# Storing the leftover tokens of a fused attention and two-layer kernel by one transfer a batch, from two issuing engines

## The chip, the cores and the metric

The kernel runs on one core of one Trainium2 chip. Its time is the device time of one execution in microseconds (us). The engines are named as the profile names them: PE (matrix multiplication) with PEld (its weight loads), DVE, ACT and POOL (the three engines for elementwise work), and SP, which here only issues transfers. Sixteen DMA engines move data between the on-chip memory and DRAM.

## The reference

Four batches (B) of eight heads, 576 tokens (S) a batch. Linear attention with 128 random features gives 2304 rows of 512 values; two gated feed-forward layers with 2048 hidden columns follow. The output is 2304 x 512 in fp32, its row being `batch * 576 + token`.

```python
q_p, k_p = (phi(q_s), phi(k_s))             # phi: exp of a projection on omega, less a maximum
kv = np.einsum('bhsm,bhsd->bhmd', k_p, v)
num = np.einsum('bhsm,bhmd->bhsd', q_p, kv)
out = num / den                              # attention; then rows (b s), columns (h d)

h = x @ w_in                                 # layer one
x = (h * np.clip(h + 3.0, 0.0, 6.0) / 6.0) @ w_out
h = x @ w_in                                 # layer two, with weights of its own
out = (h * (1.0 / (1.0 + np.exp(-1.702 * h)))) @ w_out
```

## The kernel before

A batch of 576 tokens is cut into 512 main tokens (`SM`) and 64 leftover tokens (`SL`). The main tokens of each batch are a block of their own, i = 0 to 3; the 4 x 64 leftover tokens of all batches together are a fifth block, i = B = 4, of 256 tokens. Token t of that block belongs to batch t // 64, so tokens 0 to 127 are batches 0 and 1, and 128 to 255 batches 2 and 3.

A first stretch computes the attention of batch 0, then the units of the two layers run in the order layer, batch, chunk of 128 hidden columns (16 chunks). `emit_h` (line 439) multiplies by `w_in` and applies the gate, `emit_o` (line 501) multiplies by `w_out` and adds up in PSUM, two units later. fp32 values are split into two parts, and three products are taken. The attention of the next batch is slipped in between, step by step, through `side()`.

The last pass of layer two handles batch 3 and the leftover block together (`SEGS[3]`). At its end (`tail`) the order of `emit_o` is written out by hand: the main block's last chunk first, then the leftover block's last two. The leftover block has two accumulators, d = 0 and d = 1, of 128 tokens by 512 columns each; both are finished last in the program.

`put` takes an accumulator from PSUM into the tile `ob` (line 522 on ACT for even d, line 520 on DVE for odd d) and stores it: line 524 for layer one, line 529 for a main block of layer two (128 rows of the output that follow each other), and line 534 for the leftover block. Line 534 is reached twice. All stores of `put`, and all other transfers, are issued by SP, in program order. The tile `ob` has six buffers in this stage (`lp`), so that no store waits there for an earlier one. Line 717 is the end of the program, where SP waits for the transfers still under way, and all engines meet.

Of the kernel before, what the change touches and what calls it, by code (L numbers as in the profile page):

```python
# [46 lines left out]
def performer_moe_kernel(  # L47
# [13 lines left out]
    nc = tc.nc  # L61
# [9 lines left out]
    SM = R * P  # L71
    SL = lv.shape[1] // 2
    S = SM + SL
# [392 lines left out]
    def emit_o(l, n, c, side):  # L466
# [5 lines left out]
        for c, i, N in parts:  # L472
# [7 lines left out]
            for d, ps in enumerate(oacc[l, i]):  # L480
# [27 lines left out]
                if c == NC - 1:  # L508
                    put(l, i, d, ps, per)
# [4 lines left out]
    def put(l, i, d, ps, per):  # L514
        pool, bufs = (gp, 2) if lp is None else (lp, 6)
        ob = pool.tile([P, SM], F32, tag="ob", bufs=bufs, name="ob")
        ps = ps.rearrange("p e s -> p (e s)")
        sc = 1.0 / 6.0 if l == 0 else 1.0
        if d % 2:
            nc.vector.tensor_scalar(out=ob, in0=ps, scalar1=sc, scalar2=None, op0=ALU.mult)  # L520
        else:
            nc.scalar.activation(out=ob, in_=ps, func=AF.Copy, scale=sc)
        if l == 0:
            nc.sync.dma_start(
                out=xs[i][d * per:(d + 1) * per].rearrange("e p s -> p e s"),
                in_=ob.rearrange("p (e s) -> p e s", e=per),
            )
        elif i < B:
            nc.sync.dma_start(
                out=out[i * S + d * P:i * S + (d + 1) * P, :],  # L530
                in_=ob,
            )
        else:
            nc.sync.dma_start(
                out=out.rearrange("(b s) e -> b s e", s=S)[2 * d:2 * d + 2, SM:S, :],
                in_=ob,
            )

    def split_x(t, x, kk):
        nc.scalar.copy(x[:, 0, kk, :], t[:, kk, :])  # L540
# [18 lines left out]
    for n in range(WARM):  # L559
        nc.tensor.matmul(  # L560
            out=ps.rearrange("p a m -> p (a m)"),
# [6 lines left out]
    for e in range(2):  # L568
# [5 lines left out]
            out=bd_lo[rows, e, :],  # L574
# [147 lines left out]
```

## Time and profile before

| | us |
|---|---|
| median of 3 runs | 982.69 |
| lowest and highest of the three | 978.67, 982.96 |
| the profiled execution | 980.37 |
| its span, first to last instruction | 978.6 |
| last stretch, 965.10 to the end, without work on any engine | 13.5 |

The profile's page gives the busy time of each engine, its share in 40 slices of the span, the DMA queues and the chain of work that ended last. Other views group the instructions by line, list them in order of time, tell what each waited for, and count in any stretch the DMA packets, the bytes moved and the share of the sixteen DMA engines that was busy. Times in them count from the span's start.

### The profile page before, as it was taken

The numbers are of one execution on the slowest core, as the hardware profiler recorded it, in microseconds if no ns is written. First come the engines' busy times: TensorE is split into PE (matmuls) and PEld (weight loads), VectorE is DVE, ScalarE is ACT, GpSimd is POOL, SyncE is SP. The second block draws the span as 40 slices with busy tenths as digits, with TensorE's granted clock in tenths as the row PEclk, the third lists the DMA queues.
The fourth block names the chain that finished last, engine by engine and source line by source line (L and its number), as shares of the span: only waits on it lengthen the run. The fifth ranks groups of instructions, "written<-read, shape, count | busy, mean of one in ns | idle before, by whom it ended". The sixth has DMA issues, their size and how long they took to land.

```text
span 978.6 us, 14409 instructions
## 1 busy us (share of the span) xinstructions
PE 946.1 (97%) x5626; PEld 783.8 (80%) x5626; DVE 477.7 (49%) x845; ACT 415.5 (42%) x868; POOL 152.4 (16%) x127
## 2 busy tenths in 40 slices
PE   8799999999999999999999999999999999999994
PEld 6678777788877778778888888888888888888883
DVE  7988988886776875333222222223223222322221
ACT  5976776675655665342222322222123212221221
POOL 0212322334443343030000101020002000000000
PEclk9999999999999999999999999999999999999997
DMA  6666677977788865246333384446335443422301
GB/s 196 249 226 224 214 258 247 370 266 270 270 306 281 288 227 204 86 151 211 120 124 128 129 264 140 134 148 212 131 130 175 130 144 114 150 67 86 108 1 64
DMA packets 54775, 177.23 MB, mean 181 GB/s; under 512 B 5812, under 2 KB 7476, under 8 KB 54708
## 3 DMA queue, kind: packets, MB, share of 16 engines
q1 hardware_dynamic: 54708, 176.32, 52.9%
q8 instruction: 44, 0.72, 0.3%
q14 instruction: 23, 0.19, 0.1%
HBM read 138.55 MB, written 37.75 MB: 180 GB/s over the span
## 4 chain that ended last, share of the span: by engine, by line
PE 74%; DVE 7%; DMA 7%; POOL 5%; ACT 3%; issue 3%; SPq 0%; POOLq 0%; ACTq 0%
PE ps L439 34%; PE o L501 34%; DMA ws1i<-wsn 4%; POOL wsn L211 3%; DVE w L205 3%; PE ps L225 2%; DMA ws1o<-wsn 2%; POOL w L202 2%; DVE mx L231 1%; PE ps L329 1%; ACT w L187 1%; PE ps L292 1%; DVE wtop L193 1%; ACT e L233 0%; DMA qk<-in_qk_dram 0%
## 5 line engine op out<-in xcount | busy, mean ns | idle before, releaser
L439 PE MATMUL ps<-x,wss 128*128 128x512 f32 x1152 | 287.3, 394 | 3.4 <-ACT wss L210 1.9
L439 PEld LDWEIGHTS ps<-x,wss 128*128 128x128 f32 x1152 | 212.2, 188 | 48.0 <-ACT wss L210 3.5
L457 DVE TENSOR_TENSOR ga<-ga,ps 128x512 f32<-128x512 f32 x80 | 50.8, 635 | 252.4 <-ACT ga L456 252.4
L456 ACT ACTIVATE ga<-ps 128x512 f32<-128x512 f32 x80 | 44.4, 554 | 252.3 <-PE ps L439 252.3
L501 PE MATMUL o<-gs,wss 128*128 128x512 f32 (+1 forms) x600 | 137.3, 375 | 1.3 <-ACT gs L459 1.0
L460 DVE TENSOR_TENSOR gs<-ga,gs 128x512 fp32r<-128x512 f32 (+1 forms) x160 | 109.1, 697 | 51.1 <-ACT gs L459 48.1
L501 PE MATMUL o<-wss,gs 128*128 128x512 f32 x540 | 129.8, 390 | 0.0
L501 PEld LDWEIGHTS o<-gs,wss 128*128 128x128 f32 x600 | 102.2, 189 | 20.1 <-ACT gs L459 1.3
L501 PEld LDWEIGHTS o<-wss,gs 128*128 128x128 f32 x540 | 100.7, 188 | 20.5
L459 ACT CAST gs<-ga 128x512 fp32r<-128x512 f32 (+1 forms) x160 | 91.7, 579 | 43.6 <-DVE ga L457 32.4
L202 POOL TENSOR_TENSOR w<-w,wpow 128x512 f32<-128x512 f32 x64 | 77.7, 1234 | 168.0 <-DVE wpow L197 129.1
L452 DVE SCALAR_TENSOR_TENSOR ga<-ga,ps 128x512 f32<-128x512 f32 x80 | 50.1, 629 | 109.3 <-ACT ga L451 109.1
L439 PE MATMUL ps<-x,wsh 128*128 128x512 f32 x384 | 94.7, 393 | 0.5 <-ACT wsh L210 0.5
L451 ACT ACTIVATE ga<-ps,three 128x512 f32<-128x512 f32 x80 | 51.6, 648 | 101.7 <-PE ps L439 101.5
L439 PEld LDWEIGHTS ps<-x,wsh 128*128 128x128 f32 x384 | 70.9, 188 | 15.8 <-ACT wsh L210 0.7
L501 PE MATMUL o<-gs,wsh 128*128 128x512 f32 (+1 forms) x360 | 82.9, 374 | 0.6 <-ACT gs L459 0.4
L205 DVE TENSOR_TENSOR w<-w,wtop 128x512 f32<-128x512 f32 x64 | 75.3, 1188 | 16.3 <-POOL w L202 16.3
L501 PE MATMUL o<-wsh,gs 128*128 128x512 f32 x324 | 78.5, 390 | 0.0
L233 ACT ACTIVATE e<-ps,mx 128x128 f32<-128x128 f32 x220 | 63.4, 386 | 24.6 <-DVE mx L231 24.4
L501 PEld LDWEIGHTS o<-gs,wsh 128*128 128x128 f32 x360 | 61.6, 189 | 12.2 <-ACT gs L459 1.0
L501 PEld LDWEIGHTS o<-wsh,gs 128*128 128x128 f32 x324 | 60.4, 188 | 12.3
L541 POOL TENSOR_TENSOR x<-xr,x 128x512 fp32r<-128x512 f32 x16 | 22.2, 1417 | 264.2 <-ACT x L540 264.2
(123 smaller groups left out, 963.3 us busy)
## 6 DMA issues: line engine op xcount, KB each, us to landing
wss<-ws1i SPq DMA_DIRECT2D x48, 512.0 KB, 3.2
wss<-ws1o SPq DMA_DIRECT2D x40, 512.0 KB, 3.3
wss<-ws0i SPq DMA_DIRECT2D x36, 512.0 KB, 4.9
wraw<-in_w_in_dram SPq DMA_DIRECT2D x32, 512.0 KB, 4.5
wraw<-in_w_out_dram SPq DMA_DIRECT2D x32, 512.0 KB, 5.6
wss<-ws0o SPq DMA_DIRECT2D x30, 512.0 KB, 4.2
ws1i<-wsn SPq DMA_DIRECT2D x16, 512.0 KB, 3.5
ws1o<-wsn SPq DMA_DIRECT2D x16, 512.0 KB, 3.0
```

Of the source, the lines that this page charges most:

```text
L202: nc.gpsimd.tensor_tensor(out=w[:, cols], in0=w[:, cols], in1=q[:, cols], op=ALU.mult)
L205: nc.vector.tensor_tensor(out=wj, in0=wj, in1=a[:, j * DM:(j + 1) * DM], op=ALU.add)
L211: (nc.vector if l == 0 else nc.gpsimd).tensor_tensor(out=s[:, 1], in0=wj, in1=s[:, 0].bitcast(F32), op=ALU.subtract)
L233: act = nc.scalar.activation(out=e[:, r, :], in_=ps[:, r, :], func=AF.Exp, bias=mx[:, r:r + 1])
L439: nc.tensor.matmul(out=ps, lhsT=w[:, wi, kk, :], rhs=x[:, xi, kk, :], start=(m == 0), stop=(m == 3 * NK - 1),)
L451: nc.scalar.activation(out=g, in_=ps, func=AF.Relu, bias=three)
L452: nc.vector.scalar_tensor_tensor(out=g, in0=g, scalar=6.0, in1=ps, op0=ALU.min, op1=ALU.mult)
L456: nc.scalar.activation(out=g, in_=ps, func=AF.Sigmoid, scale=1.702)
L457: nc.vector.tensor_tensor(out=g, in0=g, in1=ps, op=ALU.mult)
L459: nc.scalar.copy(s[:, 0, :], g)
L460: nc.vector.tensor_tensor(out=s[:, 1, :], in0=g, in1=s[:, 0, :].bitcast(F32), op=ALU.subtract)
L501: last = nc.tensor.matmul(out=ps[:, e, :], lhsT=lhsT, rhs=rhs, start=(c == 0 and m == 0 and per == 1), stop=(c == NC - 1 and m == 2 and e ...
```

## The change

The leftover block's store of one accumulator (128 rows of `ob`, two batches of 64 rows each, which lie 576 rows apart in the output) becomes two stores of 64 rows. The one for the even batch is issued by SP, the one for the odd batch by ACT. Line 534 is reached for d = 0 and d = 1, so two transfers become four.

```diff
         else:
-            nc.sync.dma_start(
-                out=out.rearrange("(b s) e -> b s e", s=S)[2 * d:2 * d + 2, SM:S, :],
-                in_=ob,
-            )
+            for e, eng in enumerate((nc.sync, nc.scalar)):
+                r0 = (2 * d + e) * S + SM
+                eng.dma_start(out=out[r0:r0 + SL, :], in_=ob[e * SL:(e + 1) * SL, :])
```

## Rows read from the trace of the kernel before

**Rows 1.** The page: span, busy us of PE with its share, PE and DMA by slices

```profile
span 978.6 us, 14409 instructions
PE 946.1 (97%) x5626; PEld 783.8 (80%) x5626; DVE 477.7 (49%) x845; ACT 415.5 (42%) x868; POOL 152.4 (16%) x127
...
PE   8799999999999999999999999999999999999994
...
DMA  6666677977788865246333384446335443422301
```

**Rows 2.** Busy us (x instructions) in four stretches, then granted clock, DMA share, GB/s

```profile
0.00:662.00 662.00, 643.72 (x4204) 530.06 (x4205) 394.85 (x711) 341.70 (x731) 146.92 (x123) 1.00 0.62 213
662.00:956.18 294.18, 294.18 (x1388) 247.27 (x1388) 79.42 (x129) 70.83 (x132) 5.49 (x4) 1.00 0.36 119
956.18:965.10 8.92, 8.19 (x37) 6.42 (x35) 3.42 (x6) 2.96 (x6) 0.00 (x0) 1.00 0.30 112
965.10:978.60 13.50, 0.00 (x0) 0.00 (x0) 0.00 (x0) 0.00 (x0) 0.00 (x0) 0.64 0.12 43
```

**Rows 3.** End of the chain of work that ended last: start us, us, what

```profile
956.18 8.20 PE o L501 x36
964.38 0.02 issue
964.41 0.69 DVE ob L520
```

**Rows 4.** Timeline, 960 to 979: start us, us, engine, line, names, count [idle before]

```profile
961.63 1.80 SPq L529 DMA_DIRECT2D out_dram<-ob  x4
...
963.73 0.60 ACT L522 ACTIVATE ob<-o 128x512 f32<-128x512 f32 x1 [1.63 <-PE o L501]
964.35 1.30 SPq L534 DMA_DIRECT2D out_dram<-ob  x2
964.41 0.69 DVE L520 TENSOR_SCALAR ob<-o 128x512 f32<-128x512 f32 x1 [1.89 <-PE o L501]
```

**Rows 5.** SP's own waits, 960 to 979: total us, times, longest us

```profile
SPq L717 <- DMA out_dram<-ob: 11.9, 2, 6.8
```

**Rows 6.** Line 717 in 966 to 979: ns min/median/max, first and last start us

```profile
L717 SPq EVENT_SEMAPHORE  x7: 17/28/28, 972.5 to 978.5; - x7
```

**Rows 7.** DMA packets and MB in 962 to 965.5, 965.5 to 972.2, 972.2 to 977.4

```profile
DMA packets 576, 1.05 MB, mean 300 GB/s; under 512 B 64, under 2 KB 64, under 8 KB 576
...
DMA packets 133, 0.27 MB, mean 40 GB/s; under 512 B 2, under 2 KB 2, under 8 KB 133
...
DMA packets 127, 0.26 MB, mean 49 GB/s; under 512 B 2, under 2 KB 2, under 8 KB 127
```

**Rows 8.** The columns of rows 2 around the last stores

```profile
963.00:964.00 1.00, 1.00 (x7) 0.79 (x5) 0.00 (x0) 0.27 (x1) 0.00 (x0) 1.00 1.00 367
964.00:965.00 1.00, 0.37 (x2) 0.00 (x0) 0.59 (x1) 0.32 (x1) 0.00 (x0) 1.00 1.05 393
...
972.20:977.20 5.00, 0.00 (x0) 0.00 (x0) 0.00 (x0) 0.00 (x0) 0.00 (x0) 0.50 0.13 51
```

**Rows 9.** Line 529: ns to issue, start us; its last four from issue to landing

```profile
L529 SPq DMA_DIRECT2D out_dram<-ob x4: 338/395/425, 961.6 to 963.0; - x4
...
DMA to landing us min/median/max: 2.1/2.4/2.7
```

**Rows 10.** Lines 534 and 524: ns min/median/max to issue, first and last start us

```profile
L534 SPq DMA_DIRECT2D out_dram<-ob x2: 527/597/667, 964.4 to 965.1; - x2
...
L524 SPq DMA_DIRECT2D xs<-ob x18: 319/320/1114, 191.7 to 577.8; - x18
```

**Rows 11.** DMA queues of the page, and line 164's landing, min/median/max, the trace's longest

```profile
q1 hardware_dynamic: 54708, 176.32, 52.9%
...
DMA to landing us min/median/max: 3.1/3.3/8.5
```

**Rows 12.** Timeline, 0 to 14: what the engines do first

```profile
0.74 1.28 ACT L233 ACT_TABLE_LOAD   x1 [0.74 <-PEq L709]
0.74 0.40 SPq L124 DMA_DIRECT2D qk<-in_qk_dram  x1
```

## The prediction

> **What bounds the kernel now.** I read the page first, then the stretches of the span, then the chain, the timeline and the DMA counts of the last 20 us. The page says that PE is busy for 946.1 of 978.6 us [rows 1], so nearly everywhere the time is PE's. The exception is the last slice of its row of digits, a 4. By stretches it is plain: PE works without a gap from 662.00 to 956.18, and from 965.10 to the end at 978.60 no engine does anything at all [rows 2]. That is 13.5 us, and the edited line is the one that issues the stores under way in it.
>
> The chain of work ends at 964.41 + 0.69 = 965.10 with DVE's eviction of the last accumulator [rows 3]; the chain doesn't follow the store behind it, so the reader must go on with SP. SP issues line 534's two stores from 964.35 to 965.65 [rows 4], one behind ACT's eviction of d = 0, one behind DVE's of d = 1. Then it waits in line 717 for transfers from `ob`, twice, 11.9 us in all, the longer one 6.8 us [rows 5]. So the first store is home at 965.65 + 6.8 = 972.5, which is where the first of line 717's semaphore instructions starts [rows 6], and the second 11.9 - 6.8 = 5.1 us later, at about 977.6. From there to the span's end it is 1.0 us of closing.
>
> Why are these two stores slow? The four stores of line 529 just before them carry the same 256 KB each. While those run, the DMA engines are wholly busy (share 1.00 to 1.05) and move 367 to 393 GB/s; while the second store of line 534 runs, the share is 0.13 and the rate 51 GB/s [rows 8]. A share of 0.13 of sixteen engines is 2.1 engines. 256 KB at 51 GB/s are 5.1 us, the distance of the two landings. The count of tiny packets says the same: the stretch that ends line 529's four stores has 64 packets under 512 B, sixteen a store; each of the two stretches that end a store of line 534 has 2 [rows 7]. Each finished engine leaves one such packet, as I read it, so line 529 runs on sixteen engines and line 534 on two. Line 529's destination is 128 rows; line 534's is two groups of 64 rows. I take the outermost count, two, for what limits it: that is an inference from two stores beside four, and the terms below hang on it.
>
> **The change part by part.** *Removed:* two stores on two engines, and with them the time from the last eviction's end at 965.10 to the second landing at 977.6: 12.5 us.
>
> *Added:* four stores of 64 rows, 128 KB each. No row shows a 64-row store, so I bound it by line 529, whose rows follow each other as the new ones do. Its last four landed 2.1, 2.4 (median) and 2.7 us after issue [rows 9]; the first has empty DMA engines before it, the last has three stores ahead of it. In the new kernel the pair of d = 1 is issued when DVE ends, at about 965.13. Two halves together are one store of line 529 in bytes, 256 KB, 0.67 us at 393 GB/s. The pair of d = 0, issued at 964.35, has the 0.67 us after line 529's data, which end shortly after 965, and is done by about 966.0, roughly when the data of the next pair may begin. So the last pair is nearer to the unqueued case: I take 2.1 us, landing at 965.13 + 2.1 = 967.2. The good end is a half that profits from its size alone, 2.1 - 0.33 = 1.8 us, and the bad end 2.7 us.
>
> *Moved to ACT:* two of the four issues. No row shows ACT issuing a transfer; SP's issues took 0.34 to 0.43 us on line 529 [rows 9], 0.53 to 0.67 on line 534, and at the longest 1.1 on line 524 [rows 10]. With up to 0.77 us between the two evictions' ends (964.33 and 965.10) ACT's first issue is hidden and its second costs nothing beyond SP's. With 1.1 us ACT could start its second only at 965.4, 0.3 us late, and I allow 0.6 us more for that issue itself. What is queued behind these instructions? On ACT nothing: its eviction of d = 0 at 963.73 is its last work [rows 4], and the wait for DVE's eviction, which ACT gains before its second store, holds up line 717 alone. On SP too nothing but line 717 follows. If such a store stood anywhere earlier in ACT's order, evictions and gates would queue behind it; here it can't, since it needs the last accumulators. SP loses two issues and gains two, shorter ones if anything: nothing, since PE doesn't wait for SP there.
>
> *Closing:* the 1.0 us with line 717's seven semaphore instructions on SP [rows 6] gets up to two more waits, for the two stores more. Shared out evenly that is 0.14 each; I take 0.1 in all, ends 0 and 0.3.
>
> *Sum:* the new end is 967.2 + 1.0 + 0.1 = 968.3 in place of 978.6: **10.3 us less**. Ends: 1.8 us and no added closing give 10.7; 2.7 us, an ACT late by 0.9 and 0.3 of closing give 8.6. Nothing before 963.73 is touched, so no other stretch gives or takes. What is late next is PE itself, up to 964.38, with one eviction, one store and the closing behind it, and no wait that a further edit of the stores alone could remove by more than a microsecond.
>
> **Against the rule.** By the row the halves gain since the whole is on two engines. The Trainium skill ("DMA: Bandwidth & Descriptors", section Rules for kernel authors) advises against this very edit: two transfers to disjoint partition halves serialize on the same sixteen engines, so one of 128 partitions should be used, and spreading over issuing engines only saves issue time. That presumes a whole that uses sixteen engines, which this trace contradicts with its share of 0.13 [rows 8]; by the rule taken literally the second rival below would come about. On what no row here shows, the same page (section on why a DMA increments its semaphore by 16) lets the slowest dimension's size choose the engines, so that 64 rows would get sixteen; by it the sum stays and the first rival below falls away.
>
> **The rivals.**
>
> 1. *Only eight engines serve a half.* 64 partitions are half of 128, and if a partition's place fixes its engine, a half has eight. If both halves had the same eight, the four stores' 512 KB would go at half of 393 GB/s, 2.7 us in place of 1.3: 1.4 us of the gain lost, 8.9 us saved. For it: no row excludes it. Against it: line 534's own whole covers all 128 partitions and runs on two engines, so the partition doesn't fix the engine there.
>
> 2. *The halves run one after another, each with its whole 2.1 us.* From 964.35 on, 4 x 2.1 = 8.4 us: the last is home at 972.8, the end is at 973.9, 4.7 us saved. Against it: line 529's four stores are issued within 1.8 us and land at most 2.7 us after issue [rows 4, 9], so stores overlap.
>
> 3. *The change doesn't do what it says*: a half too is confined to two engines, by something other than the count of groups. Then 512 KB still go at 51 GB/s, and the end stays at 978.6: no change. Against it: sixteen tiny packets a store of plain rows [rows 7].
>
> 4. *Slower: ACT's queue must be opened and closed.* All dynamic packets belong to a single queue, q1 [rows 11], and ACT issues nothing before. If a second queue cost a round of fetching before the first instruction or behind the last, it would stand on the path with nothing over it. The nearest price is the longest landing of the trace, 8.5 us [rows 11], twice 17 us: 6.7 us slower than before on balance. It decides the sign from 10.3 us on. Against it: SP issues its first load at 0.74, together with ACT's first instruction [rows 12], so that one queue in use shows no such cost inside the span, and outside the span lie only 980.37 - 978.6 = 1.8 us in all.
>
> **How the numbers follow.** The profiled execution took 980.37 us, so by its own time the forecast is 980.37 - 10.3 = 970.1. It lies 2.3 us below the median of the three runs (982.69). The four executions known (978.67, 980.37, 982.69, 982.96) have a mean of 981.2; less 10.3 that is 970.9, and I give 971.0. Rival 1 gives 981.2 - 8.9 = 972.3, rival 2 976.5, rival 3 981.2, rival 4 987.9. Chances: forecast 0.82, rival 1 0.07, rival 2 0.05, rival 3 0.03, rival 4 0.03. The range takes the lowest run with the largest gain, 978.67 - 10.7 = 968.0, and the highest with the smallest, 982.96 - 8.6 = 974.4; it holds the forecast and rival 1, some 0.85 with what runs may stray beyond. A measurement here can tell about 0.5%, 4.9 us, from no change: the forecast and rival 1 are beyond it (0.89), rival 2 stands at the line, half of it counted as faster: 0.91; the rest of it with rival 3 is 0.06; rival 4 is 0.03.
>
> **What would show it.** In the new profile the stretch without work behind DVE's last eviction should be 3.2 us long in place of 13.5, with a DMA share near 1 and over 300 GB/s for about 1.3 us; the four new stores should leave 64 tiny packets in place of 4; SP's wait in line 717 should be under 2 us; ACT should show two issues after 964.3, and the stretches before 963.73 should be as they are. A share near 0.5 means rival 1; 0.13 means rival 3; landings 2 us apart mean rival 2; a span that shrinks while the time doesn't means rival 4. The prediction is wrong if the outermost count isn't what confines line 534, or if an issue from ACT takes several microseconds.

## The result, and the profile after

The changed kernel takes 973.11 us (median of five runs, 969.93 to 975.92), beside 982.69 us for the kernel before. The ratio is 0.9904, with a 95% interval of 0.9881 to 0.9927: faster by 9.6 us. The profiled execution took 971.03 us, 9.3 us below the profiled one of before.

The page of the changed kernel, in the form of [rows 1]: span, busy us, and PE and DMA by slices.

```profile
span 969.2 us, 14413 instructions
...
PE 946.6 (98%) x5626; PEld 784.8 (81%) x5626; DVE 479.9 (50%) x845; ACT 416.2 (43%) x868; POOL 153.6 (16%) x127
...
PE   8899999999999999999999999999999999999998
...
DMA  6666676977788865335334374336344444422311
```

PE is busy as long as before (946.1 us there), and its last slice has risen from 4 to 8: only idle time went. The first and the last of the stretches of [rows 2], cut at the end of the last eviction, which now is at 965.38 (964.69 + 0.69, below):

```profile
0.00:662.00 662.00, 643.99 (x4203) 530.82 (x4204) 396.77 (x711) 342.02 (x731) 148.10 (x123) 0.99 0.62 213
...
965.38:969.24 3.86, 0.00 (x0) 0.00 (x0) 0.00 (x1) 0.00 (x0) 0.00 (x0) 0.69 0.52 149
```

The stretch without work fell from 13.50 to 3.86 us, 9.64 less. The last eviction ended 0.28 us later than in the profile of before, which is a difference between two executions of the same earlier work; the two together are the 9.4 us by which the span shrank.

The timeline of the end, to be read beside [rows 4], then SP's wait as in [rows 5]:

```profile
964.01 0.60 ACT L522 ACTIVATE ob<-o 128x512 f32<-128x512 f32 x1 [1.63 <-PE o L501]
964.63 1.25 SPq L536 DMA_DIRECT2D out_dram<-ob  x2
964.64 1.44 ACTq L536 DMA_DIRECT2D out_dram<-ob  x2
964.69 0.69 DVE L520 TENSOR_SCALAR ob<-o 128x512 f32<-128x512 f32 x1 [1.89 <-PE o L501]
...
SPq L716 <- DMA out_dram<-ob: 2.3, 3, 1.5
```

Both engines issue two halves each, and SP's waiting for transfers has come down from 11.9 to 2.3 us. The DMA packets behind line 529's stores, from 965.70 to the end, with the queues (packets, MB, share of sixteen engines):

```profile
DMA packets 320, 0.52 MB, mean 148 GB/s; under 512 B 64, under 2 KB 64, under 8 KB 320
...
q1 hardware_dynamic: 160, 0.26, 29.8%
q10 hardware_dynamic: 160, 0.26, 23.1%
```

64 tiny packets for four stores, where two stores had left 4 [rows 7]: each half runs on sixteen engines. SP's two go through queue q1, ACT's through a queue of their own, q10.

### The profile page after: what moved, and what is told of

It is laid out like the page before. It is cut to its first block, busy times and chain, and to the rows that moved or that the text cites. A ratio compares the mean times of both kernels' runs of the same rounds, so it can differ in the third digit from the quotient of the medians.

```text
span 969.2 us, 14413 instructions
## 1 busy us (share of the span) xinstructions
PE 946.6 (98%) x5626; PEld 784.8 (81%) x5626; DVE 479.9 (50%) x845; ACT 416.2 (43%) x868; POOL 153.6 (16%) x127
## 4 chain that ended last, share of the span: by engine, by line
PE 76%; DVE 8%; DMA 5%; POOL 4%; ACT 3%; issue 3%; SPq 0%; POOLq 0%; ACTq 0%
PE o L501 35%; PE ps L439 35%; DMA ws1i<-wsn 4%; DVE w L205 2%; PE ps L225 2%; POOL wsn L211 2%; POOL w L202 2%; DMA ws1o<-wsn 1%; DVE mx L231 1%; PE ps L329 1%; PE ps L292 1%; ACT w L187 1%; DVE wtop L193 1%; ACT e L233 1%; DVE wss L211 1%
## 5 line engine op out<-in xcount | busy, mean ns | idle before, releaser
L205 DVE TENSOR_TENSOR w<-w,wtop 128x512 f32<-128x512 f32 x64 | 77.3, 1219 | 14.9 <-POOL w L202 14.9
(123 smaller groups left out, 964.4 us busy)
```

Of the source, the lines that this page charges most:

```text
L205: nc.vector.tensor_tensor(out=wj, in0=wj, in1=a[:, j * DM:(j + 1) * DM], op=ALU.add)
```

## The experiments

Each run is judged by one measure, the stretch from the end of the last eviction to the end of the span in its profile, 13.50 us before and 3.86 after. Whole executions differ by some 4 us among themselves, while this stretch agrees within 0.1 us in the two profiles of the changed kernel (3.86 and 3.80). Rows of an experiment are, in this order, that stretch (columns of [rows 2]), the DMA packets from about 0.3 us behind its start on, when line 529's data are through, and where needed the issues (ns min/median/max) with their landing.

Theory A: the outermost count of a store's rows sets how many DMA engines serve it. Theory B: the second issuer and its queue bring the gain. Theory C: two places apart in DRAM are slow as such, or only small transfers are quick.

**The split alone.** All four halves issued by SP:

```diff
-            for e, eng in enumerate((nc.sync, nc.scalar)):
+            for e, eng in enumerate((nc.sync, nc.sync)):
```

> The four half stores of the change, all issued by SP. The measure is the stretch from the end of the last eviction to the end of the span (before 13.5 us, after 3.8). Theory A (the outermost count of the store's rows sets how many DMA engines serve it): the split alone brings the gain, 64 tiny packets from the four stores, stretch 3.6 to 4.3 us, since SP's second issue for d = 1 comes some 0.5 us later. Theory B (the second issuing engine and its queue bring the gain): 13 us or more.

```profile
964.13:968.51 4.38, 0.00 (x0) 0.00 (x0) 0.00 (x0) 0.00 (x0) 0.00 (x0) 0.88 0.59 131
...
964.50:967.00 2.50, 0.00 (x0) 0.00 (x0) 0.00 (x0) 0.00 (x0) 0.00 (x0) 1.00 0.94 200
...
DMA packets 320, 0.52 MB, mean 128 GB/s; under 512 B 64, under 2 KB 64, under 8 KB 320
...
L536 SPq DMA_DIRECT2D out_dram<-ob x4: 542/564/592, 963.4 to 965.2; - x4
DMA to landing us min/median/max: 2.3/2.3/2.4
```

4.38 us, a little above the 3.6 to 4.3 expected: the split without ACT brings 9.1 of the 9.6 us. Theory B falls. Each issue takes 0.54 to 0.59 us, so the last half is issued about 0.6 us behind the third. The second row shows a thing that comes back below: the sixteen engines are busy (share 0.94), yet move only 200 GB/s.

**The second issuer alone.** The two whole stores of before, that of d = 1 by ACT:

```diff
-            nc.sync.dma_start(
+            (nc.scalar if d else nc.sync).dma_start(
                 out=out.rearrange("(b s) e -> b s e", s=S)[2 * d:2 * d + 2, SM:S, :],
```

> The two whole stores of before, the second one issued by ACT. Theory A: 4 tiny packets, DMA share about 0.13, 512 KB at about 51 GB/s on the same two engines, stretch without work 13 to 14.5 us. Theory B: the two stores run on two queues side by side, stretch under 9 us.

```profile
963.99:977.31 13.32, 0.00 (x0) 0.00 (x0) 0.00 (x0) 0.00 (x0) 0.00 (x0) 0.62 0.12 43
...
DMA packets 260, 0.52 MB, mean 40 GB/s; under 512 B 4, under 2 KB 4, under 8 KB 260
...
L534 ACTq DMA_DIRECT2D out_dram<-ob x1: 1137/1137/1137, 964.0 to 964.0; - x1
```

13.32 us and 4 tiny packets, at a DMA share of 0.12: two queues share the same two engines. The mean rate, 40 GB/s, is below the 51 expected. ACT needed 1.14 us to issue this store, about as long as SP's longest issue on line 524 (1.11 us in [rows 10]).

**Four groups in place of two.** Two whole stores by SP; the leftover tokens are put in another order in their block when attention writes them, so that an accumulator holds 32 tokens of every batch:

```diff
-            c0 = self.b * SL
-            nc.scalar.copy(self.xl[:, :, c0:c0 + SL], ps)
+            to = self.xl.rearrange("p k (d b s) -> p k b d s", d=2, b=B)
+            nc.scalar.copy(to[:, :, self.b], ps.rearrange("p k (d s) -> p k d s", d=2))
...
+            s0 = SM + d * SL // 2
             nc.sync.dma_start(
-                out=out.rearrange("(b s) e -> b s e", s=S)[2 * d:2 * d + 2, SM:S, :],
+                out=out.rearrange("(b s) e -> b s e", s=S)[:, s0:s0 + SL // 2, :],
```

> Two whole stores by SP, but the leftover tokens stand in another order in their block, so that one accumulator holds 32 tokens of each of the four batches: 128 rows in four groups. Theory A: four engines, 8 tiny packets from the two, DMA share about 0.25, about 102 GB/s, 2.6 us a store, stretch about 7 us. Theory C (a transfer to places that lie apart in DRAM is slow as such, two groups or four): about 51 GB/s again and 13.5 us, or longer.

```profile
965.99:975.04 9.05, 0.00 (x0) 0.00 (x0) 0.00 (x1) 0.00 (x0) 0.00 (x0) 0.69 0.21 64
...
DMA packets 264, 0.52 MB, mean 60 GB/s; under 512 B 8, under 2 KB 8, under 8 KB 264
...
SPq L718 <- DMA out_dram<-ob: 7.4, 2, 4.9
...
966.25:969.00 2.75, 0.00 (x0) 0.00 (x0) 0.00 (x0) 0.00 (x0) 0.00 (x0) 1.00 0.22 31
969.00:971.00 2.00, 0.00 (x0) 0.00 (x0) 0.00 (x0) 0.00 (x0) 0.00 (x0) 0.60 0.26 99
```

8 tiny packets from two stores, a share of 0.26 (4.2 engines), 99 GB/s and 7.4 - 4.9 = 2.5 us between the landings: four engines, as theory A says, although the rows now lie in more places. The stretch is 2 us longer than the 7 expected, and the last two rows show where: in the first 2.75 us the engines are as busy (0.22) but move only 31 GB/s. More on that at the end.

**The same whole store, turned round.** Two whole stores of 256 KB by SP. The tokens of two batches alternate, and the store counts tokens first and batches second, 64 groups of two:

```diff
-            nc.scalar.copy(self.xl[:, :, c0:c0 + SL], ps)
+            to = self.xl[:, :, c0:c0 + 2 * SL].rearrange("p k (s e) -> p k e s", e=2)
+            nc.scalar.copy(to[:, :, self.b % 2], ps)
...
-                out=out.rearrange("(b s) e -> b s e", s=S)[2 * d:2 * d + 2, SM:S, :],
+                out=out.rearrange("(b s) e -> s b e", s=S)[SM:S, 2 * d:2 * d + 2, :],
```

(`c0` is `self.b // 2 * 2 * SL` here.)

> Two whole stores of 256 KB by SP as before, but the leftover tokens of two batches alternate in their block, so that a store's rows are 64 groups of two. Theory A: sixteen engines, 32 tiny packets from the two, over 350 GB/s, landing 2.1 to 2.4 us after issue, stretch from the last eviction to the end 3.1 to 3.5 us, so 0.3 to 0.7 us less than with the change, and a time of 0.989 to 0.991 of before. Theory C (two places apart in DRAM are slow as such, or only small transfers are quick): 13.5 us and no change in the time.

```profile
966.43:969.89 3.46, 0.00 (x0) 0.00 (x0) 0.00 (x1) 0.00 (x0) 0.00 (x0) 0.95 0.45 167
...
DMA packets 288, 0.52 MB, mean 164 GB/s; under 512 B 32, under 2 KB 32, under 8 KB 288
...
L535 SPq DMA_DIRECT2D out_dram<-ob x2: 546/603/660, 965.7 to 966.5; - x2
DMA to landing us min/median/max: 2.4/2.5/2.5
```

3.46 us, 32 tiny packets. Size, number of stores, issuer and places in the output are those of before; only the order of the two counts differs, and with it the order of the tokens in the tile. Theory C falls, and theory A has its fourth point (2, 4 and 64 of a count, and a plain store). The landing, 2.4 to 2.5 us, is a little later than the 2.1 to 2.4 expected. The ratio to before is 0.9904 (0.9890 to 0.9917).

**The change beside it on the same chip.**

> The changed kernel beside the others on the same chip. Theory A: stretch 3.8 us, time about 0.990 of before, 0.3 to 0.7 us behind the kernel with 64 groups of two.

```profile
965.36:969.16 3.80, 0.00 (x0) 0.00 (x0) 0.00 (x1) 0.00 (x0) 0.00 (x0) 0.96 0.51 152
```

The ratio is 0.9911 (0.9897 to 0.9925). The turned store is 0.34 us ahead in the stretch, as expected; the times don't tell the two apart.

**What the 2.1 us should have been.** Three runs take the last landing apart, which came 2.9 us after its issue. All halves by ACT (`(nc.scalar, nc.scalar)`):

> The four half stores of the change, all issued by ACT. Theory A: 64 tiny packets, stretch 3.6 to 5 us. In the changed kernel ACT's stores took 2.7 and 2.9 us from issue to landing, SP's 2.3 and 2.4. If ACT's issue itself is the slower one, all four take 2.7 us or more here and the stretch is 4.3 us or more; if the two issuers get in each other's way, they take about 2.3 us and the stretch is about 3.8.

```profile
967.77:972.20 4.43, 0.00 (x0) 0.00 (x0) 0.00 (x1) 0.00 (x0) 0.00 (x0) 0.81 0.59 130
...
L536 ACTq DMA_DIRECT2D out_dram<-ob x4: 552/577/608, 967.0 to 968.9; - x4
DMA to landing us min/median/max: 2.3/2.4/2.4
```

ACT issues and lands as SP does alone, 2.3 to 2.4 us. The stretch is longer than the 3.8 that went with that landing: the expectation forgot that one engine issues one half after the other. The turned store with that of d = 1 issued by ACT:

> As the kernel with 64 groups of two, the store of d = 1 issued by ACT. It has no other store of the same moment beside it. If ACT's issue itself is slower, landing 2.6 to 2.9 us after issue and the stretch 0.4 us longer than with SP; if the two issuers only got in each other's way, 2.1 to 2.4 us.

```profile
963.45:967.01 3.56, 0.00 (x0) 0.00 (x0) 0.00 (x1) 0.00 (x0) 0.00 (x0) 0.68 0.44 162
...
L535 ACTq DMA_DIRECT2D out_dram<-ob x1: 658/658/658, 963.5 to 963.5; - x1
DMA to landing us min/median/max: 2.5/2.5/2.5
```

The stretch is 0.1 us longer than with SP, not 0.4. The landing, 2.5 us, lies between the two ranges expected, but SP's stores of this shape took 2.4 to 2.5 too. So ACT's issue isn't what cost the time. And plain stores of 128 rows at the same point of the program:

```diff
-            nc.sync.dma_start(
-                out=out.rearrange("(b s) e -> b s e", s=S)[2 * d:2 * d + 2, SM:S, :],
-                in_=ob,
-            )
+            nc.sync.dma_start(out=out[2 * d * S:2 * d * S + P, :], in_=ob)
```

> The two whole stores of before, 256 KB each by SP, go to 128 rows of the output that follow each other (over the first rows of batches 0 and 2), so the leftover tokens' own rows are not written and the output is not the reference's. Theory A: sixteen engines, 32 tiny packets from the two, stretch without work 3.0 to 3.5 us. It also measures the term that was set too low, 2.1 us from issue to landing: if the shape of the halves' rows made their issue longer (0.47 to 0.67 us against 0.34 to 0.43 of line 529), these two take 0.34 to 0.43 us to issue and 2.1 us to land; if it is their place at the end, 0.5 to 0.7 us and 2.4 to 2.5 us.

```profile
963.84:966.92 3.08, 0.00 (x0) 0.00 (x0) 0.00 (x0) 0.00 (x0) 0.00 (x0) 1.00 0.50 187
...
L534 SPq DMA_DIRECT2D out_dram<-ob x2: 332/332/333, 963.1 to 963.9; - x2
DMA to landing us min/median/max: 2.0/2.1/2.1
```

0.33 us to issue, 2.0 to 2.1 to land: the shape of the stores, not their being the last, makes issue and landing longer.

**A last eviction in two halves.** The turned store, and the last accumulator evicted by ACT and DVE in halves of columns, each stored by itself:

> As the kernel with 64 groups of two, and the last accumulator is evicted in two halves of columns, by ACT and DVE side by side, each stored on its own by SP and ACT (128 KB, rows of 1 KB). Theory A: the eviction takes about 0.4 us in place of 0.69, and the last landing is bound by the issue and not by the data, so the end comes 0.3 us earlier at most; if halves of a store cost the 0.5 us that the changed kernel shows over line 529's stores, it comes 0.2 us later. Neither can be told in the time, only in the trace.

```profile
967.22:970.53 3.31, 0.00 (x0) 0.00 (x0) 0.00 (x1) 0.00 (x0) 0.00 (x0) 0.80 0.46 160
...
958.16 8.20 PE o L502 x36
...
966.38 0.38 ACT L524 ACTIVATE ob<-o 128x256 f32<-128x256 f32 x1
966.80 0.42 DVE L527 TENSOR_SCALAR ob<-o 128x256 f32<-128x256 f32 x1 [2.30 <-ACT ob L524]
```

The stretch is 0.15 us shorter than that of the turned store, but the two evictions of one accumulator ran one after the other (0.38, then 0.42 us) and not side by side, so the 0.3 us of the shorter eviction weren't there. Since the eviction itself got longer, the stretch behind it is no fair measure here. From PE's end, at 958.16 + 8.20 = 966.36, to the end of the span it is 4.17 us; in the kernel with the turned store alone PE ends at 965.72, and it is 4.17 us too:

```profile
957.52 8.20 PE o L502 x36
```

So the halves of columns gained nothing. The ratio to before, 0.9887 (0.9872 to 0.9902), is the lowest of the kernels that ran more than once, but its interval overlaps those of the change and of the turned store, and the profiles show no gain behind it.

## Why the prediction was right

**The forecast.** 971.0 us with 10.3 us less; measured 973.11 and 9.6 less, inside the range of 968.0 to 974.4, and faster beyond the 4.9 us that can be told. Of the 2.1 us between the two times 0.7 is gain that didn't come; the rest comes from the time of before, taken as 981.2 from four executions where the median of five is 982.69.

**Two engines, because of the outermost count.** This was an inference, and everything hung on it. It is now shown: 2 groups give 2 tiny packets a store, 4 give 4, 64 groups of two give 16, at 51, 99 and (in [rows 8], for the plain store) 367 to 393 GB/s. The turned store changes only the order of the counts, with the tokens put in that order, and takes all of the gain.

**What goes.** The 12.5 us from the last eviction to the last landing went as worked out.

**What comes: the mis-sized term.** The landing of the last pair was set at 2.1 us, with 2.7 as the bad end; it took 2.9, as the two engines' halves show in the changed kernel, ACT's first and then SP's:

```profile
L536 ACTq DMA_DIRECT2D out_dram<-ob x2: 570/620/669, 964.6 to 965.4; - x2
DMA to landing us min/median/max: 2.7/2.8/2.9
...
L536 SPq DMA_DIRECT2D out_dram<-ob x2: 474/510/546, 964.6 to 965.4; - x2
DMA to landing us min/median/max: 2.3/2.4/2.4
```

The step that failed is "Two halves together are one store of line 529 in bytes, 256 KB, 0.67 us at 393 GB/s", and with it that the pair of d = 0 "is done by about 966.0". The halves are one store in bytes, but neither in issuing nor in rate. A half alone takes 0.54 to 0.61 us to issue and 2.3 to 2.4 to land, by SP as by ACT, where a plain store of twice its bytes takes 0.33 and 2.0 to 2.1. And with all four halves issued by SP the busy engines moved 200 GB/s (the row of that run above), by ACT 202 in 968.50 to 970.50. The turned stores, 256 KB each, were at 344 GB/s with the same share:

```profile
967.00:968.50 1.50, 0.00 (x0) 0.00 (x0) 0.00 (x0) 0.00 (x0) 0.00 (x0) 1.00 0.93 344
```

So a half keeps the engines as long as a whole store. In the changed kernel the packets of the two queues (packets, MB, share; a half is 0.13 MB), in 965.50 to 966.50, to 967.00 and to 968.00, show what came of it:

```profile
q1 hardware_dynamic: 83, 0.14, 67.2%
q10 hardware_dynamic: 1, 0.00, 0.5%
...
q10 hardware_dynamic: 79, 0.13, 68.3%
q1 hardware_dynamic: 47, 0.07, 36.8%
...
q10 hardware_dynamic: 80, 0.13, 47.1%
q1 hardware_dynamic: 48, 0.07, 23.0%
```

SP's first half (q1) runs until about 966.5, ACT's first (q10) behind it until 967.0, so the pair of d = 0 is done 1.0 us later than forecast. In the last pair too ACT's half ends last. ACT's halves land 0.3 and 0.6 us behind SP's of the same moment; for the last one the 0.6 us and the 0.2 us that a half alone takes longer are the 0.8 us missing. The rates while SP's first and then ACT's first ran:

```profile
966.00:966.50 0.50, 0.00 (x0) 0.00 (x0) 0.00 (x0) 0.00 (x0) 0.00 (x0) 1.00 0.91 176
966.50:967.00 0.50, 0.00 (x0) 0.00 (x0) 0.00 (x0) 0.00 (x0) 0.00 (x0) 0.87 1.05 393
```

The low rate of SP's half doesn't come from the two issuers holding each other up, since one issuer alone shows it as well. What does cause it stays open. The pace of issuing would fit: 128 KB in 0.54 to 0.61 us are 215 to 243 GB/s (an estimate from the issues above), and the half that ran behind another issuer's, ACT's first, went at full rate. No run tests it.

**Moved to ACT.** Right that nothing on ACT queues behind it. ACT's own issue was no cost: with SP alone the stretch is 4.38, with ACT alone 4.43, with both 3.80 to 3.86. So beside the split the second issuer is worth 0.5 to 0.6 us, what is left of a halved row of issues when ACT's halves come behind SP's.

**Closing.** The last landing is at 965.4 + 2.9 = 968.3, and 0.9 us of closing follow, not 1.1: no cost of two stores more shows there. This 0.2 us goes against the 0.8 of the landing, so that the gain is off by 0.7 only.

**The rivals.** Rival 1 (eight engines a half): sixteen tiny packets a half, no. But the rate that it gave, half of 393 GB/s, did come, with all sixteen engines busy. Rival 2 (one after another at 2.1 us each): the halves' data did run largely one after another, but the landings of one pair lie 0.3 and 0.6 us apart, not 2.1. The Trainium skill's advice against two halves ("DMA: Bandwidth & Descriptors", Rules for kernel authors) holds in this measure: the turned whole store beats the two halves by 0.34 us. It doesn't hold against a whole that runs on two engines. Rival 3: no. Rival 4 (ACT's queue must be opened): the time outside the span is 971.03 - 969.2 = 1.8 us as before, and PE's busy time in the first 662 us is 643.99 beside 643.72; no cost shows.

**The signs named.** 64 tiny packets and two issues on ACT came; the stretch was 3.86, not 3.2; SP's wait 2.3, not under 2; the data took some 2.3 us (965.6 to 967.9) at uneven rates, not 1.3; all three come from the one term, the halves' data.

## What to carry to other kernels

When the profile ends in a stretch without work, look at the DMA share there: a share of 0.13 is two of sixteen engines, and the tiny packets count them per transfer. Write the store so that its outermost count is large, by turning the order of the counts or the order of the data, or else by splitting it; the order of the data was the better of the two here, by 0.34 us of the stretch. Counts between 4 and 64 were not tried. In this kernel it matters for the transfer that ends the program, where nothing else covers it, and what can be gained is the uncovered time alone.

## What the runs showed of the hardware that was not expected

The first store on few engines started slowly here. In the kernel with four groups the first store, issued at 965.24, was home at 971.5 (4.9 us after SP's two issues ended at 966.58), 6.2 us in all, its successor 2.5 us later with the same bytes; the share was 0.22 in its first 2.75 us, but the rate 31 GB/s in place of 99. Before the change the first store likewise took 972.5 - 964.4 = 8.1 us [rows 6, 10], and the second landed 5.1 behind it. The packets were long in that time. Every such store followed busy engines and had a second one issued behind it, so no run tells what makes it slow.

A store of 64 rows moved at about half the rate of one of 128, 200 GB/s beside 344, with the DMA engines as busy.

Of the last stores' issues those of 128 plain rows were the shortest, 0.33 us; the others can't be told apart: 0.54 to 0.61 for 64 plain rows from one engine, 0.55 to 0.66 for 64 groups of two, 0.53 to 0.67 for two groups of 64 on SP. The 1.14 us of ACT's is a single issue, and stores of 128 rows on line 524 reach 1.11 us too [rows 10], so it can't be put down to the shape. What makes an issue longer stays open.

Nearly the same work reaches its last eviction between 963.45 and 967.77 in the profiles shown here. That spread, 4.3 us, is as large as that of the times of before (978.67 to 982.97), so a change at the end of a kernel is read from the stretch behind the last work with far more certainty than from the time.
